# First scores by head halves: k on its own queue, all eight PSUM banks, and a new order for three batches

## The chip, the cores and the metric

The kernel runs on one core of a Trainium2 chip. The metric is device time in microseconds. A core has a matrix engine (TensorE, PE in the profile; its weight loads are PEld), a vector engine (VectorE, DVE), a scalar engine for functions of one argument (ScalarE, ACT), a general one (GpSimd, POOL) and one that only issues transfers (SyncE, SP). Each has its own queue of instructions and works through it in order. Semaphores make one wait for another. Matrix results go to PSUM, a memory of eight banks of 128 partitions x 512 FP32. Transfers from main memory are issued by GpSimd or by the sync queue and are carried out by 16 DMA engines.

## The reference

Causal attention with a window of 64 keys (batch 8, 8 heads, 576 positions, 64 columns a head), then a gated feed-forward layer (4608 tokens, 512 columns, 1536 hidden).

```python
scores = scale * np.matmul(q, k.transpose(0, 1, 3, 2))
rel = pos[:, None] - pos[None, :]
scores = np.where((rel >= 0) & (rel < 64), scores, -1e9)
scores = scores - np.max(scores, axis=-1, keepdims=True)
attn = np.exp(scores)
attn = attn / (np.sum(attn, axis=-1, keepdims=True) + 1e-09)
x = np.matmul(attn, v)              # heads side by side: [4608, 512]
out = (np.maximum(x @ w_gate, 0.0) * (x @ w_val)) @ w_out
```

## The kernel before

Attention is cut into 24 units of 192 query positions (three a batch), the feed-forward layer into 12 tiles of 384 tokens, two units each. A scheduler of its own fixes the order: `W.at(t, fn)` puts a piece of work on a heap, and while the feed-forward matmuls are emitted the clock `W.clock` moves and due pieces are emitted between them. The times `t` only order things; nothing waits for them on the chip.

Loads of q and k go over GpSimd's queue, which turns FP32 into FP16 on the way, one transfer for each half (`hh`) of the eight heads. VectorE transposes 32 x 32 blocks:

```python
def qk_load(b, name, hh):
    tile_ = nat[b, name, hh] = a_in.tile([128, S // 32 * D], FP16, name=f"{name}{hh}", bufs=2)
    src = (q if name == "q" else k)[b, G * hh:G * hh + G]
    nc.gpsimd.dma_start(tile_, src.rearrange("h (i j) d -> (h i) (j d)", i=32))

def qk_trans(b, name, hh):
    ...
    nc.vector.transpose(dst.rearrange("p (i j) -> p j i", i=32), src)
```

A unit: scores of four heads side by side on TensorE (`u_st`, the 64 columns of a head summed in two parts `dh`; both head halves in one bank), the exponential on ScalarE, the window mask as a product on VectorE (units 0 and 1 instead start from a large negative bias that TensorE adds, `u_bias`), P times V and the row sums on TensorE (`u_pv`), then the division:

```python
def u_st(u):
    ...
    for hh in range(2):
        for w in range(2):
            for dh in range(2):
                for g in range(G):
                    rows = slice(32 * g, 32 * g + 32)
                    nc.tensor.matmul(d["st"][g][:, (2 * hh + w) * 128:(2 * hh + w + 1) * 128],
                                     kT[rows, hh, ...], qT[rows, hh, ...], ...)

def u_exp(u, g):
    nc.scalar.activation(d["p"][g]..., d["st"][g], ACT.Exp, scale=scale)      # 512 columns

def u_copy(u, n):  nc.scalar.copy(d["xs"][:, c], d["pv"][c][:, 0])            # P times V, unnormalized
def u_sum(u, half): nc.vector.transpose(to[:, c], d["pv"][c][:, 1])           # row sums
def u_back(u):      # reciprocal, and transpose back
def u_norm(u):      nc.vector.tensor_tensor(xt[...], d["xs"], rs, MUL)
```

PSUM is held by two pools: `f_ps` with four tiles of one bank (tag "h") and `a_ps` with two tiles of two banks (tag "a"). Unit 0 scores into the four of `f_ps`, later units into `a_ps`. `heat(n)` issues n matmuls of zeros that keep TensorE active. The program:

```python
for name, hh in (("k", 0), ("k", 1), ("q", 0), ("q", 1)):
    qk_load(0, name, hh)
...
heat(12, units[1]["st"][0])
bands(); constants(); v_ones(1, nc.vector)     # masks on GpSimd, constants on VectorE
W.at(5.85, band_bias)
W.at(6.2, lambda: v_load(0)); W.at(6.3, lambda: v_load(1))
W.at(6.4, lambda: w_load(*G3[0], 15.0))        # then V3[0], G3[1], V3[1], G3[2], V3[2]
...
W.at(11.0, lambda: heat(8))
plan_unit(0, 10.2, ...); plan_unit(1, 10.8, ...); plan_unit(2, 24.0, *fast)
plan_unit(3, 45.3, *fast); plan_unit(4, 53.0); plan_unit(5, 60.5, *fast)
...
W.advance(15.7)
ready(1); hidden(0, 0, U, 0, 4, 4)             # projections of tile 0, tokens 0 to 191
ready(2); hidden(0, U, TT, 0, 4, 4)            # tokens 192 to 383
hidden(0, 0, TT, 4, NF, 4)
output_by_rows(0)
ready(3); hidden(1, 0, U); output(1, (0,))
ready(4); hidden(1, U, TT); output(1, (1, 2))
for t in range(2, NU // 2):
    ready(2 * t + 2); hidden(t, 0, TT)
    (output if t < NU // 2 - 1 else output_last)(t)
```

`hidden` makes the gate and value projections (512 columns of x against 128 of the weights, four matmuls a block), the relu on ScalarE and the product on VectorE; `output` the last projection.

Of the kernel before, what the change touches and what calls it, by code (L numbers as in the profile page):

```python
# [9 lines left out]
FP32 = mybir.dt.float32  # L10
FP16 = mybir.dt.float16
ACT = mybir.ActivationFunctionType
# [30 lines left out]
def kernel(  # L43
# [121 lines left out]
        src = (q if name == "q" else k)[b, G * hh:G * hh + G]  # L165
        nc.gpsimd.dma_start(tile_, src.rearrange("h (i j) d -> (h i) (j d)", i=32))

    def qk_trans(b, name, hh):

        src = nat.pop((b, name, hh)).bitcast(FP32).rearrange("p (j e) -> p j e", e=32)  # L170
        dst = qTs[b % 2][:, hh] if name == "q" else kTs[b % 2][:, hh, 64:64 + S]
        dst = dst.bitcast(FP32).rearrange("p c o -> p (c o)")
        nc.vector.transpose(dst.rearrange("p (i j) -> p j i", i=32), src)  # L173

    def v_load(u):
        b, uu = divmod(u, UB)
# [7 lines left out]

        nc.vector.tensor_copy(v16s[u % UB][0:64, 0, :, 0:64], v16s[u % UB - 1][64:128, 1, :, 0:64])

    def u_bias(u):

        d = units.setdefault(u, {})
        if "st" not in d:  # L190
            st_tiles(u)
        d["biased"] = True
        for g in range(G):
            nc.tensor.matmul(d["st"][g].rearrange("p (h c) -> p h c", h=2), ident,
                             bias.rearrange("p w c -> p (w c)")[:, None, :].to_broadcast([128, 2, 256]),
                             start=True, stop=False, skip_group_check=True)

    def heat(n, to=None):

        if to is None:  # L200
            to = f_ps.tile([128, 512], FP32, name="h0", tag="h")
        for _ in range(n):
            nc.tensor.matmul(to, zero[:, 0:128], zero, start=True, stop=True)  # L203

    def st_tiles(u):
        d = units.setdefault(u, {})
        if u == 0:
            d["st"] = [f_ps.tile([128, 512], FP32, name="st", tag="h") for _ in range(G)]
        else:
            halves = [a_ps.tile([128, 2, 512], FP32, name="st", tag="a") for _ in range(2)]  # L210
            d["st"] = [halves[g // 2][:, g % 2] for g in range(G)]

    def u_st(u):
        d = units.setdefault(u, {})
        kT, qT = kTs[(u // UB) % 2], qTs[(u // UB) % 2]
        biased = "biased" in d
        if not biased:
            st_tiles(u)
        ks = U * (u % UB)
        for hh in range(2):  # L220
            for w in range(2):
                for dh in range(2):
                    for g in range(G):
                        rows = slice(32 * g, 32 * g + 32)
                        nc.tensor.matmul(  # L225
                            d["st"][g][:, (2 * hh + w) * 128:(2 * hh + w + 1) * 128],
                            kT[rows, hh, ks + 128 * w:ks + 128 * w + 128, dh],
                            qT[rows, hh, ks + 64 * w:ks + 64 * w + 128, dh],
                            start=(dh == 0 and not biased), stop=(dh == 1),
                            skip_group_check=biased)  # L230
        d["p"] = [None] * G
        return 0.65

    def u_exp(u, g):
        d = units[u]
        d["p"][g] = a_p.tile([128, 2, 256], FP16, name="p")
        nc.scalar.activation(d["p"][g].rearrange("p h c -> p (h c)"), d["st"][g], ACT.Exp, scale=scale)  # L237

    def u_mask(u, g):
        p = units[u]["p"][g]  # L240
        nc.vector.tensor_tensor(  # L241
            p, p, mask.rearrange("p w c -> p (w c)")[:, None, :].to_broadcast([128, 2, 256]), MUL)

    def u_pv(u):
        if u > 1:
            return u_pv_wide(u)
        d = units[u]
        v16 = v16s[u % UB]
        if u == 0:
            d["pv"] = [f_ps.tile([128, 2, U], FP32, name="pv", tag="h") for c in range(NC)]  # L250
        else:
            halves = [a_ps.tile([128, 2, 512], FP32, name="pv", tag="a") for _ in range(2)]
            d["pv"] = [halves[c % 2][:, c // 2, 0:2 * U].rearrange("p (s c) -> p s c", s=2) for c in range(NC)]
        for c in (0, 2, 1, 3):
            for s in range(2):
                for w in range(2):
                    for e in range(2):
                        h = 2 * c + e
                        nc.tensor.matmul(
                            d["pv"][c][64 * e:64 * e + 64, s, 64 * w:64 * w + 128],  # L260
                            v16[:, w, h, 0:64] if s == 0
                            else (ones0 if u % UB == 0 and w == 0 else ones),
                            d["p"][h % G][:, h // G, 128 * w:128 * w + 128],
                            start=(s == 0 and w == 0), stop=(s == 1 and w == 1),
                            skip_group_check=True)
        return 1.2
# [18 lines left out]
    def u_copy(u, n):  # L285
        d = units[u]
        if "xs" not in d:
            d["xs"] = a_n.tile([128, NC, U], FP32, name="xv", bufs=2)
        if u < 2:
            c = (0, 2, 1, 3)[n]  # L290
            nc.scalar.copy(d["xs"][:, c], d["pv"][c][:, 0])
        else:
            for e in range(2):
                rows = slice(64 * e, 64 * e + 64)
                nc.scalar.copy(d["xs"][rows, n::2], d["pv"][n][rows, :, e, 0:U])  # L295

    def u_sum(u, half):
# [2 lines left out]
            d["sT"] = a_n.tile([128, NC, U // 32, 32], FP32, name="sT", bufs=1)  # L300
        to = d["sT"].rearrange("p g b c -> p g (b c)")
        if u < 2:
            for c in (half, half + 2):
                nc.vector.transpose(to[:, c], d["pv"][c][:, 1])
        else:
            for e in range(2):
                nc.vector.transpose(to[64 * e:64 * e + 64, half::2],  # L307
                                    d["pv"][half][64 - 64 * e:128 - 64 * e, :, e, 0:U])
# [138 lines left out]
                    out_evac(t, op, sub)  # L447

    with tc.manual_schedule():
        for name, hh in (("k", 0), ("k", 1), ("q", 0), ("q", 1)):  # L450
            qk_load(0, name, hh)
        warm = consts.tile([128, 2], FP32)
        nc.vector.memset(warm, 0.0)
        nc.scalar.activation(warm[:, 1:2], warm[:, 0:1], ACT.Exp)
        zero = consts.tile([128, 512], FP16)
        nc.vector.memset(zero, 0.0)
        st_tiles(1)
        heat(12, units[1]["st"][0])
        bands()
        constants()  # L460
        v_ones(1, nc.vector)
        W.at(5.85, band_bias)
        G3, V3, O3 = ([(wt, src, f0, f0 + 4) for f0 in (0, 4, 8)]
                      for wt, src in ((wg, moe_w_gate), (wv, moe_w_val), (wo, moe_w_out)))
        W.at(6.2, lambda: v_load(0))
        W.at(6.3, lambda: v_load(1))
        W.at(6.4, lambda: w_load(*G3[0], 15.0))
        W.at(6.5, lambda: w_load(*V3[0], 17.6))
        W.at(6.6, lambda: w_load(*G3[1], 20.2))
        W.at(9.9, lambda: w_load(*V3[1], 22.8))  # L470
        W.at(9.9, lambda: w_load(*G3[2], 25.4))
        W.at(9.9, lambda: w_load(*V3[2], 28.0))
        W.at(12.3, lambda: v_load(2))
        W.at(13.6, lambda: w_load(*O3[0], 32.5))
        W.at(13.7, lambda: w_load(*O3[1], 35.1))
        plan_batch(0, None, (4.5, 5.9, 7.3, 8.8))
        plan_batch(2, 37.6, (71.0, 72.4, 73.8, 75.2))
        plan_batch(1, None, (37.5, 39.0, 42.6, 44.0))
        W.at(13.8, lambda: qk_load(1, "k", 0))
        W.at(13.8, lambda: qk_load(1, "k", 1))  # L480
        W.at(13.9, lambda: w_load(*O3[2], 40.6))
        W.at(14.0, lambda: qk_load(1, "q", 0))
        W.at(14.0, lambda: qk_load(1, "q", 1))
        W.at(14.1, lambda: v_load(3))
        W.at(30.0, lambda: v_load(4))
        W.at(30.1, lambda: v_load(5))
        W.at(6.2, lambda: u_bias(0))
        W.at(6.3, lambda: u_bias(1))
        W.at(11.0, lambda: heat(8))
        W.at(13.5, lambda: v_before(1))  # L490
        W.at(21.0, lambda: v_ones(2, nc.vector))
        W.at(18.0, lambda: v_before(2))
        W.at(21.0, lambda: v_ones(0, nc.vector))
        W.at(22.0, k_zeros)
        fast = 0.8, 1.5, 3.9, (4.1, 5.3), (4.2, 5.4, 6.4, 7.5), 0.5
        plan_unit(0, 10.2, 0.7, None, 2.7, (4.4, 4.4, 4.4, 4.4), (3.4, 3.3, 4.2, 4.7), 0.5)
        plan_unit(1, 10.8, 2.1, None, 4.2, (5.2, 5.2, 5.3, 5.3), (4.7, 4.6, 5.0, 5.5), 0.5)
        plan_unit(2, 24.0, *fast)
        plan_unit(3, 45.3, *fast)
        plan_unit(4, 53.0)  # L500
        plan_unit(5, 60.5, *fast)
        T = 71.5
        early, late = (-7.4, -6.0, -4.6, -3.2), (-20.3, -18.9, -17.5, -16.1)
        for t in range(3, NU // 2):
            for u, at, tr in ((2 * t, T + 0.5, early), (2 * t + 1, T + 13.2, late)):
                if u % UB == 0 and u > 2 * UB:
                    plan_batch(u // UB, at + tr[0] - 10, [at + x for x in tr])
            plan_unit(2 * t, T + (6.5 if t == 3 else 0.5))
            plan_unit(2 * t + 1, T + (15.5 if t == 3 else 13.2), copy=(4.7, 5.8), norm=(4.8, 5.9, 6.9, 8.0))
            T += 26.525  # L510
        W.advance(15.7)
        ready(1)
        hidden(0, 0, U, 0, 4, 4)
        ready(2)
# [44 lines left out]
```

The softmax here doesn't subtract the row's maximum and nothing guards it: scores larger than these inputs give would overflow.

## Time and profile before

| what | value |
|---|---|
| median of three runs | 346.7 us (345.4 to 347.64) |
| span of the profiled execution | 346.2 us |
| TensorE busy | 331.1 us, 96% |
| VectorE busy | 250.7 us, 72% |
| ScalarE busy | 182.2 us, 53% |
| first projections of tile 0, tokens 0 to 191 | at 20.86 us |
| the same for tokens 192 to 383 | at 24.27 us |

In rows of the timeline the columns are start, length, engine, line, operation, what is written and read, the shape, and the count; in brackets the idle time ahead and what ended it. In the chain they are start, length, engine and work. Matmuls overlap each other, so that the length of a row exceeds what its instructions cost one after another; starts are safer to compare than busy times.

### The profile page before, as it was taken

What the parts mean: (1) busy time and instruction counts of PE and PEld (TensorE: products, weight loads), DVE (VectorE), ACT (ScalarE), POOL (GpSimd) and SP (SyncE); (2) the same over time, 40 slices, a digit from 0 to 9 for tenths busy, and PEclk for the clock granted to TensorE, in tenths of its full rate; (3) what the DMA queues carried; (4) which work ended last, traced back from release to release, by engine and by line L of the source; (5) the groups of instructions that cost most, each with busy time, mean ns of one, the idle gap of its engine ahead of it and who ended that gap; (6) DMA issues with size and microseconds to landing.
All of it is one profiled execution on the core that took longest, in us unless ns stands there. A gap on an engine that the chain in (4) does not pass through costs nothing.

```text
span 346.2 us, 7305 instructions
## 1 busy us (share of the span) xinstructions
PE 331.1 (96%) x2936; PEld 199.5 (58%) x2936; DVE 250.7 (72%) x450; ACT 182.2 (53%) x375; POOL 66.7 (19%) x101
## 2 busy tenths in 40 slices
PE   7669899999998999999999999999999999999996
PEld 2366467955654555655665655664664664664653
DVE  5397948897897883888879864878969964865430
ACT  1356346744755555565564565564664763763322
POOL 8822421420120410420120410420110200000000
PEclk9899999999999999999999999999999999999999
DMA  7999998790351951972333864665306501001002
GB/s 129 174 205 197 202 163 160 86 175 31 25 67 57 134 80 70 119 80 91 25 24 100 87 94 103 67 111 114 24 2 111 43 2 61 32 0 62 31 2 91
DMA packets 59666, 29.70 MB, mean 86 GB/s; under 512 B 46065, under 2 KB 51057, under 8 KB 59633
## 3 DMA queue, kind: packets, MB, share of 16 engines
q0 software_dynamic: 54160, 19.80, 52.5%
q1 hardware_dynamic: 5328, 9.37, 7.2%
q8 instruction: 23, 0.38, 0.5%
q14 instruction: 11, 0.08, 0.1%
q10 hardware_dynamic: 144, 0.07, 0.1%
HBM read 39.58 MB, written 9.44 MB: 142 GB/s over the span
## 4 chain that ended last, share of the span: by engine, by line
PE 81%; DVE 12%; DMA 2%; issue 2%; ACT 1%; POOL 1%; ACTq 0%; DVEq 0%; POOLq 0%
PE h L384 51%; PE op L398 20%; PE pv L277 5%; PE st L225 4%; DVE sT L307 2%; DMA q<-in_q_dram 2%; DVE qT L173 2%; DVE xt L322 2%; DVE kT L173 1%; DVE g_sb L372 1%; DVE rs L316 1%; PE h L203 1%; PE op L430 1%; DVE p L241 1%; ACT r_sb L369 1%
## 5 line engine op out<-in xcount | busy, mean ns | idle before, releaser
L384 PE MATMUL h<-xt,wg 128*128 128x384 f16 (+1 forms) x640 | 116.6, 310 | 3.9 <-DVE xt L322 3.9
L384 PE MATMUL h<-xt,wv 128*128 128x384 f16 (+1 forms) x640 | 116.6, 310 | 0.2 <-ACT r_sb L369 0.2
L372 DVE TENSOR_TENSOR g_sb<-r_sb,h 128x384 f16<-128x384 f32 x144 | 78.0, 548 | 36.5 <-PE h L384 30.6
L369 ACT ACTIVATE r_sb<-h 128x384 f32<-128x384 f32 x144 | 70.9, 496 | 56.2 <-PE h L384 48.8
L398 PE MATMUL op<-wo,g_sb 128*128 128x512 f16 x420 | 93.2, 379 | 1.3 <-DVE g_sb L372 0.8
L384 PEld LDWEIGHTS <-wg 128*128 128x128 f16 x640 | 59.4, 98 | 37.7 <-DVE xt L322 3.1
L384 PEld LDWEIGHTS <-wv 128*128 128x128 f16 x640 | 59.7, 98 | 32.2 <-issue 0.5
L181 POOL DMA_DIRECT2D v<-in_v_dram x48 | 40.4, 847 | 192.0 <-PE pv L277 185.0
L398 PEld LDWEIGHTS <-g_sb 128*128 128x128 f16 x420 | 40.9, 98 | 49.3 <-issue 1.7
L237 ACT ACTIVATE p<-st 128x512 f16<-128x512 f32 x96 | 52.1, 606 | 21.7 <-PE st L225 20.0
L307 DVE STREAM_TRANSPOSE sT<-pv 64x384 f32<-64x384 f32 x88 | 51.1, 580 | 11.5 <-PE pv L277 9.9
L405 ACT COPY o_sb<-op 128x512 f32<-128x512 f32 x35 | 20.5, 586 | 59.6 <-PE op L398 59.6
L241 DVE TENSOR_TENSOR p<-p,mask 128x512 f16<-128x512 f16 x88 | 34.0, 420 | 24.6 <-ACT p L237 24.6
L295 ACT COPY xv<-pv 64x384 f32<-64x384 f32 x88 | 41.6, 473 | 18.8 <-DVE sT L307 8.8
L316 DVE STREAM_TRANSPOSE rs<-rT 128x768 f32<-128x768 f32 x24 | 23.5, 978 | 0.8
L277 PE MATMUL pv<-p,v 128*128 128x128 f16 x352 | 23.7, 219 | 0.4 <-DVE p L241 0.3
L322 DVE TENSOR_TENSOR xt<-xv,rs 128x768 f16<-128x768 f32 x24 | 22.8, 948 | 1.3 <-DVE rs L316 0.5
L277 PEld LDWEIGHTS <-v 128*128 128x128 f16 x352 | 21.5, 98 | 3.3 <-DVE p L241 0.5
L173 DVE STREAM_TRANSPOSE kT<-k 128x576 f32<-128x576 f32 x16 | 19.6, 1244 | 2.0 <-DMA k<-in_k_dram 1.8
L173 DVE STREAM_TRANSPOSE qT<-q 128x576 f32<-128x576 f32 x16 | 19.1, 1241 | 2.2 <-DMA q<-in_q_dram 2.1
L225 PE MATMUL st<-qT,kT 32*128 32x128 f16 x768 | 16.2, 218 | 4.1 <-DVE qT L173 4.1
L225 PEld LDWEIGHTS <-kT 32*128 32x128 f16 x768 | 11.8, 94 | 11.7 <-issue 11.7
(45 smaller groups left out, 71.5 us busy)
## 6 DMA issues: line engine op xcount, KB each, us to landing
out_dram<-o_sb SPq DMA_DIRECT2D x35, 256.0 KB, 2.0
v<-in_v_dram POOLq DMA_DIRECT2D x38, 128.0 KB, 3.9
k<-in_k_dram POOLq DMA_DIRECT2D x16, 288.0 KB, 6.6
q<-in_q_dram POOLq DMA_DIRECT2D x16, 288.0 KB, 8.4
wg<-in_moe_w_gate_dram POOLq DMA_DIRECT2D x3, 512.0 KB, 10.9
wv<-in_moe_w_val_dram POOLq DMA_DIRECT2D x3, 512.0 KB, 12.7
wo<-in_moe_w_out_dram POOLq DMA_DIRECT2D x3, 512.0 KB, 17.1
v<-in_v_dram POOLq DMA_DIRECT2D x10, 64.0 KB, 3.3
```

The source lines that it names most:

```text
L173: nc.vector.transpose(dst.rearrange("p (i j) -> p j i", i=32), src)
L181: nc.gpsimd.dma_start(v16[p0:128, w, :, 0:64], v[b, :, k0 + p0:k0 + 128].rearrange("h p d -> p h d"))
L225: nc.tensor.matmul(d["st"][g][:, (2 * hh + w) * 128:(2 * hh + w + 1) * 128], kT[rows, hh, ks + 128 * w:ks + 128 * w + 128, dh], qT[rows, h ...
L237: nc.scalar.activation(d["p"][g].rearrange("p h c -> p (h c)"), d["st"][g], ACT.Exp, scale=scale)
L241: nc.vector.tensor_tensor(p, p, mask.rearrange("p w c -> p (w c)")[:, None, :].to_broadcast([128, 2, 256]), MUL)
L277: nc.tensor.matmul(d["pv"][c % 2][:, c // 2, e, 64 * w:64 * w + 128], v16[:, w, 128 * h - 64 * e:128 * h - 64 * e + 128], d["p"][h % G][:, ...
L295: nc.scalar.copy(d["xs"][rows, n::2], d["pv"][n][rows, :, e, 0:U])
L307: nc.vector.transpose(to[64 * e:64 * e + 64, half::2], d["pv"][half][64 - 64 * e:128 - 64 * e, :, e, 0:U])
L369: nc.scalar.activation(part(r_sb), part(h1), ACT.Relu)
L372: nc.vector.tensor_tensor(g_sb[:, f:f + w, c0:c1], part(r_sb), part(h2), MUL)
L384: nc.tensor.matmul(h[:, b * n:b * n + n], wt[:, c, (f + b) * 128:(f + b) * 128 + 128], xt[:, c, c0:c1], start=(c == 0), stop=(c == NC - 1))
L398: nc.tensor.matmul(op, g_sb[:, f, bass.ds(sub * 128, 128)], wo[:, f], start=(f == 0), stop=(f == NF - 1))
```

## The change

It is for the start of the kernel and for the first batches. Five parts:

- k of batch 0 comes as FP32 over the sync queue, beside q over GpSimd's. ScalarE rounds it to FP16 in two parts a head half, and VectorE transposes each part.
- Unit 0 is scored by head halves: half 0 into the four banks of `f_ps`, half 1 into the four of `a_ps`. Each half has exponentials of 256 columns. P times V of the first two column chunks needs only head half 0. Unit 1 takes two banks of each pool.
- Warming matmuls are 256 wide, accumulate zeros into the spare half of a bank, and lie between the bias and the scores of unit 0, no longer ahead of its P times V.
- The third piece of wo is loaded ahead of batch 1's k and q instead of between them.
- Later units are planned earlier, and transposes of batches 1 and 2 stand elsewhere: one k transpose of batch 2 now lies at 50.0, near unit 4.

The core of the diff:

```diff
+    def k_first(hh):
+        k32 = nat["k32", hh] = x_sb.tile([128, S // 32 * D], FP32, name="k32", bufs=2)
+        nc.sync.dma_start(k32, k[0, G * hh:G * hh + G].rearrange("h (i j) d -> (h i) (j d)", i=32))
+
+    def k_round(hh, part, parts):
+        n = S // 32 * D // parts
+        if part == 0:
+            nat[0, "k", hh] = a_in.tile([128, S // 32 * D], FP16, name=f"k{hh}", bufs=2)
+        nc.scalar.copy(nat[0, "k", hh][:, n * part:n * part + n], nat["k32", hh][:, n * part:n * part + n])
...
     def st_tiles(u):
...
         if u == 0:
-            d["st"] = [f_ps.tile([128, 512], FP32, name="st", tag="h") for _ in range(G)]
+            d["st"] = [[one("st") for _ in range(G)]]
+            halves = [two("st") for _ in range(2)]
+            d["st"].append([halves[g // 2][:, g % 2] for g in range(G)])
+        elif u == 1:
+            half = two("st")
+            d["st"] = [[half[:, 0], half[:, 1], one("st"), one("st")]] * 2
...
-        for name, hh in (("k", 0), ("k", 1), ("q", 0), ("q", 1)):
-            qk_load(0, name, hh)
+        for hh in range(2):
+            k_first(hh)
+        for hh in range(2):
+            qk_load(0, "q", hh)
...
+        for hh in range(2):
+            for part in range(2):
+                k_round(hh, part, 2)
+        W.at(5.0, lambda: qk_trans(0, "k", 0, 0, 9))
+        W.at(5.1, band_bias)
+        W.at(5.2, lambda: qk_trans(0, "k", 0, 9, 18))
+        W.at(7.0, lambda: qk_trans(0, "q", 0))
+        W.at(8.6, lambda: qk_trans(0, "k", 1, 0, 9))
+        W.at(8.7, lambda: qk_trans(0, "k", 1, 9, 18))
+        W.at(9.9, lambda: qk_trans(0, "q", 1))
...
-        W.at(13.7, lambda: w_load(*O3[1], 35.1))
-        plan_batch(0, None, (4.5, 5.9, 7.3, 8.8))
-        plan_batch(2, 37.6, (71.0, 72.4, 73.8, 75.2))
-        plan_batch(1, None, (37.5, 39.0, 42.6, 44.0))
-        W.at(13.8, lambda: qk_load(1, "k", 0))
-        W.at(13.8, lambda: qk_load(1, "k", 1))
-        W.at(13.9, lambda: w_load(*O3[2], 40.6))
-        W.at(14.0, lambda: qk_load(1, "q", 0))
+        W.at(12.7, lambda: w_load(*O3[1], 33.8))
+        W.at(12.8, lambda: w_load(*O3[2], 36.4))
+        plan_batch(1, None, (37.5, 39.0, 40.4, 41.8))
+        W.at(13.0, lambda: qk_load(1, "k", 0))
...
-        W.at(11.0, lambda: heat(8))
+        W.at(5.3, lambda: u_bias(0))
+        W.at(5.4, lambda: heat(10, units[0]["spare"], False))
+        W.at(8.7, lambda: u_st(0, (0,)))
+        W.at(9.5, lambda: heat(8, units[0]["spare"], False))
+        W.at(11.0, lambda: u_st(0, (1,)))
+        for g in range(G):
+            W.at(9.6 + 0.05 * g, lambda g=g: u_exp(0, g, 0))
+            W.at(11.1 + 0.05 * g, lambda g=g: u_exp(0, g, 1))
+            W.at(12.0 + 0.05 * g, lambda g=g: u_copy(0, g))
+            W.at(12.3 + 0.05 * g, lambda g=g: u_exp(1, g))
+        W.at(11.4, lambda: u_pv(0, (0, 1)))
+        W.at(11.45, lambda: u_bias(1, (2, 3)))
+        W.at(11.5, lambda: u_pv(0, (2, 3)))
+        W.at(11.6, lambda: u_bias(1, (0, 1)))
+        W.at(11.7, lambda: u_st(1))
+        W.at(11.9, lambda: u_sum(0, 0))
...
-        plan_unit(3, 45.3, *fast)
-        plan_unit(4, 53.0)
-        plan_unit(5, 60.5, *fast)
-        T = 71.5
+        plan_unit(3, 42.5, *fast)
+        plan_unit(4, 50.0)
+        plan_unit(5, 58.0, *fast)
+        T = 68.4
...
-                if u % UB == 0 and u > 2 * UB:
+                if u == 2 * UB:
+                    plan_batch(2, 36.9, (50.0, T + 0.3, T + 1.7, T + 3.1))
+                elif u % UB == 0:
                     plan_batch(u // UB, at + tr[0] - 10, [at + x for x in tr])
-            plan_unit(2 * t, T + (6.5 if t == 3 else 0.5))
-            plan_unit(2 * t + 1, T + (15.5 if t == 3 else 13.2), copy=(4.7, 5.8), norm=(4.8, 5.9, 6.9, 8.0))
+            plan_unit(2 * t, T + (5.0 if t == 3 else 0.5))
+            plan_unit(2 * t + 1, T + 13.2, copy=(4.7, 5.8), norm=(4.8, 5.9, 6.9, 8.0))
...
-        W.advance(15.7)
+        W.advance(13.7)
```

## The prediction

> **What bounds the kernel now.** I began with the chain that ended last, by share of the span, because it says at once which engine sets the time.
>
> ```profile
> PE 81%; DVE 12%; DMA 2%; issue 2%; ACT 1%; POOL 1%; ACTq 0%; DVEq 0%; POOLq 0%
> ```
>
> Four fifths are TensorE. That part is a steady stream of projections and can't be shortened by a reordering, so what the change can win lies in the other fifth. The chain in order of time, from 0 to 41 us, shows where the biggest piece of it is (start, length, what):
>
> ```profile
> 3.04 8.03 DMA q<-in_q_dram
> 11.10 1.27 DVE qT L173
> 12.41 1.23 PE st L225 x48
> 13.64 3.09 PE h L203 x8
> 16.73 0.36 PE pv L259 x8
> 17.12 1.19 DVE sT L304 x4
> 18.33 0.32 DVE rT L314
> 18.67 0.99 DVE rs L316
> ...
> 19.76 0.96 DVE xt L322
> ```
>
> The second q half lands at 11.07; then follow its transpose, the scores, eight warming matmuls, P times V, and VectorE's normalization. The third view, the timeline, tells when projections start, for tokens 0 to 191 and then for 192 to 383:
>
> ```profile
> 20.86 1.48 PE L384 MATMUL h<-xt,wg 128*128 128x192 f16 x16 [1.69 <-DVE xt L322]
> ...
> 24.27 1.49 PE L384 MATMUL h<-xt,wg 128*128 128x192 f16 x16 [0.61 <-DVE xt L322]
> ```
>
> So 24.27 us pass before TensorE has all of tile 0 to work on, with only 192 tokens of the first four column blocks done by then. The fourth view, TensorE's own timeline after that, shows what else it loses:
>
> ```profile
> 40.26 7.93 PE L398 MATMUL op<-wo,g_sb 128*128 128x512 f16 x36 [0.82 <-DVE g_sb L372]
> ...
> 58.19 0.59 PE L398 MATMUL op<-wo,g_sb 128*128 128x512 f16 x2 [0.52 <-ACT r_sb L369]
> ...
> 71.14 0.82 PE L277 MATMUL pv<-p,v 128*128 128x128 f16 x8 [0.31 <-DVE p L241]
> ...
> 106.31 0.82 PE L384 MATMUL h<-xt,wg 128*128 128x384 f16 x4 [1.57 <-DVE xt L322]
> ```
>
> I compared starts with the sum of the instructions ahead of them (a 384-column matmul each 0.163 us, a score tile 0.57, a P-times-V group 0.90). Between 24.27 and 106.31 TensorE loses 1.3 us by 40.26, 0.7 by 58.7, 0.8 by 72.8 and 1.5 at 106.31: 4.3 us. After 106.31 I find nearly nothing.
>
> **What the Trainium skill says.** "DMA: Bandwidth & Descriptors", section "SWDGE vs HWDGE vs iDMA": a transfer that changes the type must be issued by GpSimd. So k on the sync queue arrives as FP32, and an engine has to round it. The same page, "Issuing engines are not separate DMA queues": all issuers share the 16 DMA engines. The trace agrees that these are busy: share 1.06 over the first 11 us. A second queue therefore shortens GpSimd's issuing and starts data earlier, but makes no bandwidth. "ScalarE: Activation LUTs", section "What ACT_TABLE_LOAD costs": 186 ns + 0.833 ns a column, about 93 ns overlapped between neighbours. For 512 columns that gives 613 and 520 ns; the trace has 600 ns for one and 3.05 us for six, 508 each. It agrees, so I use it for 256 columns: 306 ns each in a row, an estimate. "TensorE: Matmul & The Clock Gate", section "What's actually happening": the clock halves after an idle window of some 3.4 us and returns after a busy one. Here eight warming matmuls took 3.15 us, 0.39 each, and the granted clock was 0.50 from 13 to 16 us, after TensorE had been almost idle from 8.3 to 12.4. It agrees.
>
> **Part 1, loads.** GpSimd issues q at 1.31 instead of at 2.52; k goes beside it. Its mask work moves up by the two issues removed (2 x 0.62 = 1.2 us), and so do the v and weight issues. Bytes read up to the second q stay the same: four of 590 KB, which at twice the 195 GB/s that the windows show (they count the FP16 written) take 1.5 us each. Before, the first k landed at 5.05, the first q at 8.55, the second at 11.07. If the two queues share and the sync queue starts 0.5 us sooner, I put k half 0 at 4.9, q half 0 at 6.5 to 7, k half 1 at 7.8, q half 1 at 9.5 to 10 (it was the last of four before too, and v's small packets delayed it). ScalarE's rounding is four copies of 576 columns, by the same formula 0.57 us each, and VectorE transposes in halves of 0.63; both are done by about 10. What ends last remains q half 1: at 9.9, 1.2 us earlier.
>
> **Part 2, unit 0.** From q half 1 the new path is: transpose 1.27 (row above) and 0.05 of waiting; 16 score matmuls 0.4; four exponentials of 256 columns 1.3, against four of 512 at 2.05 before; so all weights of unit 0 exist 3.1 us after landing, at 13.0. Head half 0 has been scored and exponentiated in the wait, and the first two P-times-V chunks run beside the second half's exponentials. The eight 512-column warming matmuls are gone from this place. Before, the exponentials of unit 0 ended near 14.9 (12.84 + 2.05), yet P times V began at 16.66: the warming cost 1.8 us. The new 256-column ones lie in the wait for q.
>
> After 13.0: the ScalarE queue does copies of the first chunks, then VectorE's last two row sums, about 1.45 us; reciprocal 0.33, back transpose 1.0, xt 1.0: xt(0) at 16.8. On TensorE, scores of unit 1 are issued behind the P times V of unit 0; its exponentials follow the four copies, about 14.75, and last 2.05; its P times V comes ahead of the projections in the queue and ends at 17.6. So projections start at 17.6, not 20.86: 3.3 us. Unit 1's row sums (1.2), reciprocal, back transpose and xt end at 20.6, and the first two projection groups (2.8 us) fill nearly all of that time. Tile 0 is complete at 20.65 against 24.27: **3.6 us**. The weights: the first gate and value pieces were in by 16.7 and 19.5 (GpSimd's waits); 1.2 us earlier they are just in time.
>
> **Part 3, batch 1 and after.** The last wo piece ahead of batch 1 changes nothing in the total to land: wo was needed 5.2 us after 40.26, and q of batch 1 landed near 45, over 4 us before unit 3's scores at 50.43. The order after keeps some 2 us of that. What matters is VectorE, in the order in which the built kernel issues its instructions. Unit 7 moves up, its P times V now precedes the 36 output matmuls (7.8 us), and two rather than three transposes lie ahead of its xt. Row sums 2.4, two transposes 2.5, one product 0.55, normalization 2.3: 7.75 us in 8.4. The 1.5 us at 106.31 should go. But one batch-2 k transpose, 1.25 us, now lies ahead of unit 4's four mask products. In the trace those end 8.3 us after unit 3's P times V starts; with the transpose some 9.2, where TensorE comes after 7.4 to 8.1. I put the stalls there at 1.35, instead of 0.7, and at unit 5 at 1.0, instead of 0.8. At the first output group I leave 1.4: the gate products still queue on VectorE behind row sums and xt. Sum 3.8 against 4.3: **0.4 us** won.
>
> Sum: 3.6 + 0.4 = 4.0, less 0.1 for issue costs not seen: 346.7 - 3.9 = **342.8 us**.
>
> **Rivals.** (a) Weights become the bound. The DMA engines work without pause from 3 to 50 us, and the value piece for the first group lands at 18.2 by my estimate where 19.0 is needed. If the loads win only 0.3 us, TensorE waits 0.5 there: about 343.5. Speaking for it: share over 1 in every window; against: later pieces lead their use by 5 us before and by over 2 after. (b) Two queues interleave, q half 1 lands at 11 as before: then only the structure counts, 2.4 + 0.4: 343.9. (c) TensorE is cold when projections start, since it idles from about 14.5 to 16.9: half speed for up to 3 us, 1.5 us lost, about 344.3. Against: an idle 1.7 us ahead of 20.86 left the clock at 1.00. (d) Unit 4's masks cost nothing, because VectorE idles before them more than I count, and all later stalls go: 341. (e) VectorE's blocked queue spreads the stall to units 5 and 6: 345.
>
> **Range and chances.** The prologue is worth 2.4 to 4.3 by (a) to (c), the middle -1.2 to 2 by (d) and (e). Together 340.5 to 345.5. Faster by over 2% needs 6.9 us: 0.06. Slower by over 2% needs a new wait of 11 us that I see nowhere: 0.01.
>
> **What would show it.** Right: projections start at 17 to 18, tile 0's second half at 20 to 21.3, no idle above 0.3 us ahead of tile 4's first projections, P times V of unit 4 waiting on the mask product by up to 1 us, and the work from there as long as before, 239.9 us. Wrong: q landing after 10.5; a wait on a wv load; clock below 0.9 after 17 us; an op wait of over 2 us near 37; exponentials of 256 columns above 0.35 us apart.

## The result and the profile after

The changed kernel takes 342.81 us (median of four runs, 342.74 to 344.84), the kernel before in the same comparison 347.1 (345.4 to 347.64). The ratio is 0.9896, with an interval of 0.9852 to 0.994: faster by 1.0%. The prediction said 342.8, so the sum was right. The terms were not all right, and the profile shows it at once. Its span is 343.1 us, against 346.2 before.

On the page of the changed kernel, the chain that ended last by engine is still four fifths TensorE (80%, before 81%), and VectorE has a point less (11%, before 12%).

```profile
PE 80%; DVE 11%; issue 4%; DMA 2%; POOL 1%; ACT 1%; ACTq 0%; DVEq 0%; POOLq 0%
```

The timeline of the changed kernel, start of the program:

```profile
7.21 1.26 DVE L184 STREAM_TRANSPOSE qT<-q 128x576 f32<-128x576 f32 x1 [0.80 <-DMA q<-in_q_dram]
...
9.66 1.26 DVE L184 STREAM_TRANSPOSE qT<-q 128x576 f32<-128x576 f32 x1
...
10.97 0.41 PE L246 MATMUL st<-qT,kT 32*128 32x128 f16 x16 [1.06 <-DVE qT L184]
...
11.41 1.21 ACT L262 ACTIVATE p<-st 128x256 f16<-128x256 f32 x4 [1.26 <-PE st L246]
...
12.08 0.29 PE L287 MATMUL pv<-p,v 128*64 128x128 f16 x2 [0.52 <-DMA v<-in_v_dram]
...
13.91 0.42 PE L287 MATMUL pv<-p,v 128*64 128x128 f16 x4
...
19.08 1.50 PE L412 MATMUL h<-xt,wg 128*128 128x192 f16 x16
...
22.31 1.49 PE L412 MATMUL h<-xt,wg 128*128 128x192 f16 x16 [0.41 <-DVE xt L350]
```

q half 1 is transposed at 9.66 instead of 11.10, and the four exponentials end at 12.62. So far the prediction holds (9.9 and 13.0). Then the chain loses time: P times V waits for v until 12.08, and four of its matmuls take 0.42 us from 13.91 on. In the kernel before four took less:

```profile
16.91 0.28 PE L259 MATMUL pv<-p,v 128*64 128x128 f16 x4
```

Projections start at 19.08 and 22.31, where 17.6 and 20.65 were predicted. The stages of the two kernels, by busy time of each engine and the granted TensorE clock (PEclk), tell why. The kernel before:

```profile
8.00:12.00 4.00, 0.73 (x18) 0.36 (x17) 2.16 (x2) 0.00 (x0) 4.00 (x6) 1.00 2.43 144
12.00:16.00 4.00, 3.59 (x54) 1.83 (x54) 0.65 (x2) 3.05 (x6) 3.17 (x5) 0.59 1.39 188
```

The changed kernel:

```profile
8.00:12.00 4.00, 2.09 (x44) 1.45 (x42) 2.80 (x4) 1.80 (x7) 3.80 (x6) 1.00 2.65 136
12.00:16.00 4.00, 3.92 (x52) 2.03 (x54) 1.80 (x5) 1.58 (x6) 2.49 (x4) 0.57 1.25 206
```

The first busy column is TensorE; PEclk is the third number from the right. In both kernels the clock falls to about 0.58 from 12 to 16 us, after a stretch in which TensorE waited for q. This execution of the changed kernel did not escape it. Most others did: the runs list the mean granted clock, and the four at 0.998 to 1.000 have spans of 341.0 to 341.1; only the profiled one has 0.995 and 343.1.

After the start, the lines of TensorE's timeline that answer to those of the kernel before:

```profile
38.57 1.02 PE L426 MATMUL op<-wo,g_sb 128*128 128x512 f16 x4 [0.22 <-DVE g_sb L400]
39.90 6.20 PE L426 MATMUL op<-wo,g_sb 128*128 128x512 f16 x28 [0.31 <-DVE g_sb L400]
...
49.46 0.42 PE L246 MATMUL st<-qT,kT 32*128 32x128 f16 x16 [0.37 <-DVE qT L184]
...
61.28 1.39 PE L305 MATMUL pv<-p,v 128*128 128x128 f16 x16
...
70.53 0.49 PE L305 MATMUL pv<-p,v 128*128 128x128 f16 x6 [0.35 <-DVE p L266]
...
103.41 0.81 PE L412 MATMUL h<-xt,wg 128*128 128x384 f16 x4
```

The idle 1.57 us ahead of tile 4's first projections is gone. From 22.31 to 103.41 it takes 81.10 us, before (24.27 to 106.31) 82.04. From there to the end it takes 239.7, before 239.9: little happened there.

### The profile page after: what moved, and what is told of

It reads as the page before. It is cut to its first block, busy times and chain, and to the rows that moved or that the text cites. A ratio compares the mean times of both kernels' runs of the same rounds, so it can differ in the third digit from the quotient of the medians.

```text
span 343.1 us, 7364 instructions
## 1 busy us (share of the span) xinstructions
PE 332.7 (97%) x2950; PEld 201.2 (59%) x2950; DVE 251.5 (73%) x452; ACT 186.7 (54%) x383; POOL 65.7 (19%) x99
## 4 chain that ended last, share of the span: by engine, by line
PE 80%; DVE 11%; issue 4%; DMA 2%; POOL 1%; ACT 1%; ACTq 0%; DVEq 0%; POOLq 0%
PE h L412 48%; PE op L426 21%; PE pv L305 6%; DVE sT L335 3%; PE st L246 3%; DVE g_sb L400 2%; DMA v<-in_v_dram 2%; DVE qT L184 2%; DVE xt L350 1%; DVE rs L344 1%; DVE p L266 1%; DVE kT L184 1%; PE op L458 1%; PE pv L287 1%; PE st L206 1%
## 5 line engine op out<-in xcount | busy, mean ns | idle before, releaser
L260 ACT ACTIVATE p<-st 128x512 f16<-128x512 f32 x92 | 49.9, 604 | 11.6 <-PE st L246 11.4
L184 DVE STREAM_TRANSPOSE kT<-k 128x576 f32<-128x576 f32 (+1 forms) x18 | 19.8, 1119 | 1.9 <-ACT k L177 1.8
```

The source lines that it names most:

```text
L184: nc.vector.transpose(dst.rearrange("p (i j) -> p j i", i=32)[:, j0:j1], src[:, j0:j1])
```

## The experiments

Two theories that the profile leaves open. A, mine: the earlier q and the scoring by head halves shorten the start, and unit 7's place the middle. D: much of the gain is that TensorE's clock is halved less often during the wait for q. Then the kernels must be compared at the same clock. In the text below "full clock" means runs with a mean granted clock above 0.996, "halved" those with 0.995 or less; nearly all of the difference lies in the first 24 us. The kernel before, in 68 runs that accompany the experiments, was halved in 45, with a median span of 345.4, and at full clock in 23, with 343.6 (one more run, slow at 348.8, is left out). The changed kernel: 341.1 at full clock (four), 343.1 halved (one). Spans at full clock of one kernel spread by up to 1.1 us.

**start_only.** The changed start, and the order of the kernel before from the first projections of tokens 192 to 383:

```diff
-        plan_unit(3, 42.5, *fast)
-        plan_unit(4, 50.0)
-        plan_unit(5, 58.0, *fast)
-        T = 68.4
+        plan_unit(3, 43.3, *fast)
+        plan_unit(4, 51.0)
+        plan_unit(5, 58.5, *fast)
+        T = 69.5
```

(and unit 2, units 6 and 7, the transposes and the weights' planned times likewise, each 2.0 below the kernel before, so that TensorE's order is that of the kernel before).

> The changed kernel's start (k on the sync queue, unit 0 by head halves, warming matmuls moved), but from the first projection of the second token half on TensorE's order is that of the kernel before. Theory A (the start carries the gain, the middle under 1 us): about 343.7, 3.0 to 3.6 us below the kernel before, with a stall of some 1.5 us ahead of tile 4's first projections back. Rival B (the start gives back its gain to a cold TensorE and to the wait for v; the middle carries it): 345.5 or more.

343.92 us, ratio 0.9927 (0.9902 to 0.9951). Full clock 342.0 (five), 1.6 us below the kernel before; halved 343.5 (one). In its profile, whose clock was 1.00, projections of the second half start at 20.26, and the stall is back, on TensorE's timeline:

```profile
20.26 1.50 PE L412 MATMUL h<-xt,wg 128*128 128x192 f16 x16 [0.41 <-DVE xt L350]
...
102.27 0.82 PE L412 MATMUL h<-xt,wg 128*128 128x384 f16 x4 [1.57 <-DVE xt L350]
```

Theory A's number. The start does carry most of it, but at equal clock less than the 3.0 to 3.6 that A gave it.

**middle_only.** The start before, the order after, and wo ahead of batch 1:

```diff
-        T = 71.5
+        T = 70.4
...
-                if u % UB == 0 and u > 2 * UB:
+                if u == 2 * UB:
+                    plan_batch(2, 38.9, (52.0, T + 0.3, T + 1.7, T + 3.1))
+                elif u % UB == 0:
...
-            plan_unit(2 * t, T + (6.5 if t == 3 else 0.5))
+            plan_unit(2 * t, T + (5.0 if t == 3 else 0.5))
```

(units 2 to 5 and 7 likewise.)

> The kernel before's start, and the changed kernel's order on TensorE from there on, with wo ahead of batch 1. Theory A: 0.4 to 0.9 us below the kernel before, so about 346.3. Rival B: 2 us or more below.

345.85 us, ratio 0.9972 (0.9956 to 0.9988). Full clock 342.9 (seven), 0.7 below; halved 344.4 (15), 1.0 below. So 15 of 22 were halved, as often as in the kernel before: the share goes with the start. The two parts nearly add at full clock: 1.6 + 0.7 = 2.3, against 2.5 together. Against the nine full-clock runs of the same comparison alone (343.9) they are 1.9 and 1.0, so such differences are good to some 0.3 us.

**warm.** More work for TensorE in its waits:

```diff
-        W.at(9.5, lambda: heat(8, units[0]["spare"], False))
+        W.at(9.5, lambda: heat(18, units[0]["spare"], False))
...
-        W.at(11.45, lambda: u_bias(1, (2, 3)))
+        for _ in range(2):
+            W.at(11.3, lambda: u_bias(1, (2, 3)))
```

> The changed kernel with 18 instead of 8 warming matmuls in the wait for the second q half, and with the bias of unit 1's last two banks issued twice and ahead of unit 0's first P times V, where TensorE waits for v. Theory A: the granted clock stays at 1.00 from 12 to 16 us (0.50 to 0.61 in the profile of the changed kernel), P times V of unit 0 and the scores of unit 1 run at full speed, the second token half starts at 20.3 to 20.8 instead of 22.31, and the profiled span is 341.0, 2 us below that of the changed kernel's profile; the median, about 342.8, hardly moves, because its other runs were warm already. Rival: the clock makes no difference because v and ScalarE set the time; then the second half starts at 22 again.

343.45 us, ratio 0.9907 (0.9884 to 0.993). Clock 1.00 from 12 to 16 us and the second half at 20.90, 1.41 earlier than the halved profile of the changed kernel; the rival's 22 is out. But the full-clock span is 341.6, 0.5 above the changed kernel's. The doubled bias ended at 12.3 and P times V came behind it, 1.31 us after half 1's scores began (11.01 to 12.32); in start_only it came 0.35 after them.

**k_gpsimd.** k of batch 0 as before:

```diff
-        for hh in range(2):
-            k_first(hh)
-        for hh in range(2):
-            qk_load(0, "q", hh)
+        for name, hh in (("k", 0), ("k", 1), ("q", 0), ("q", 1)):
+            qk_load(0, name, hh)
...
-        for hh in range(2):
-            for part in range(2):
-                k_round(hh, part, 2)
```

> The changed kernel, but k of batch 0 again over GpSimd's queue, in FP16, with no rounding on ScalarE; the rest as changed. Theory A (the sync queue is worth the 1.4 us that q lands earlier): q half 1 lands at 11 and the time is 1.0 to 1.6 us above the changed kernel, 344.0. Rival C (the 16 DMA engines are the bound, so v of unit 0 lands when it landed and the wait for it takes the place of the wait for q): under 0.5 us above, 343.2.

343.79 us, ratio 0.992 (0.9891 to 0.9948). Full clock 342.0 (five): 0.9 above the changed kernel. q half 1 is transposed at 10.95 here and at 9.66 in the changed kernel's profile, but single executions differ by as much: wo_back, with the changed kernel's loads, has it at 10.67. So the runs decide, and the rival's 0.5 is too small. The sync queue is worth about 0.9 us.

**before_warm.** The kernel before, kept busy in its wait (the first part lies in `u_st`):

```diff
         for hh in range(2):
+            if u == 0 and hh == 1:
+                u_bias(1)
+                u_bias(1)
...
-        W.at(6.3, lambda: u_bias(1))
+        for _ in range(3):
+            W.at(6.3, lambda: u_bias(1))
```

> The kernel before, with TensorE kept busy while it waits for q: the bias of unit 1 is issued five times instead of once (two extra ahead of unit 0's scores, two between its head halves), into the same banks, so that nothing else changes. Theory D (in the kernel before the clock is halved from 12.8 to 16.8 us in most executions, the eight warming matmuls then take 3.15 us instead of 1.7 and delay P times V, and 1.5 to 2 us of the change's gain are just that it is halved less often): granted clock 1.00 in the profile, second token half at 22.3 to 22.8 instead of 24.27, span 343.6 to 344.2, median 345.4. Rival A (the exponentials and the order set the start): second half at 23.7 or later, median 346.5 or more.

346.71 us, ratio 1.0018 (1.0006 to 1.0029). A miss for D's number, and instructive. Its warming matmuls and first P times V on TensorE's timeline:

```profile
13.56 1.89 PE L203 MATMUL h<-zero 128*128 128x512 f16 x8 [0.22 <-ACT p L240]
15.37 0.30 PE L262 MATMUL pv<-p,v 128*64 128x128 f16 x4
```

Its stages:

```profile
12.00:14.00 2.00, 1.78 (x54) 1.03 (x53) 0.26 (x1) 1.09 (x3) 2.00 (x4) 1.00 1.29 178
14.00:16.00 2.00, 2.00 (x29) 1.10 (x29) 0.17 (x1) 1.95 (x4) 1.56 (x3) 1.00 1.24 206
16.00:18.00 2.00, 1.54 (x50) 1.26 (x44) 1.93 (x6) 1.89 (x6) 0.38 (x1) 1.00 1.24 206
18.00:20.00 2.00, 0.43 (x5) 0.44 (x6) 1.89 (x5) 0.08 (x1) 0.74 (x1) 0.96 1.24 206
20.00:22.00 2.00, 2.00 (x14) 1.84 (x13) 1.83 (x5) 1.46 (x5) 0.17 (x1) 0.50 1.24 207
```

The clock is full where it was halved before, and P times V starts at 15.37 instead of 16.66: by the starts, the eight warming matmuls take 1.8 us instead of 3.1. Then the wait for xt leaves TensorE at 0.43 of 2 us, and the clock is halved from 20 us on, under the projections. Nine of 22 runs were halved (345.7). At full clock (13) it takes 344.8, 1.2 above the kernel before. The added bias is in the way: in its profile q half 1 is transposed from 9.92 to 11.18, but half 1's scores, behind the bias in TensorE's order, start at 12.47. So this run shows what the clock does to the warming matmuls; it does not show what the clock alone costs the kernel before.

**late_half0** and **late_half0b.** Head half 0 not scored ahead, and its exponentials later too. The first edit:

```diff
-        W.at(8.7, lambda: u_st(0, (0,)))
+        W.at(10.95, lambda: u_st(0, (0,)))
...
-            W.at(9.6 + 0.05 * g, lambda g=g: u_exp(0, g, 0))
+            W.at(11.02 + 0.01 * g, lambda g=g: u_exp(0, g, 0))
```

> The changed kernel, but head half 0 of unit 0 is scored only when q half 1 has landed, ahead of half 1, and its exponentials with it. Theory A (scoring by halves takes four exponentials, 1.2 us, off the path from q): 1.0 to 1.3 us above the changed kernel, 343.9. Rival (P times V waits for v until 11.6 to 12 anyway, which hides most of them): under 0.6 above.

343.66 us, ratio 0.9922 (0.9893 to 0.995). The edit did not do what it was for: half 0's scores stood behind the first warming matmuls only and still ran at 8.91. Its full-clock span is 341.1 (three), that of the changed kernel, and three of six were halved. The second edit puts half 1's scores first in the order:

```diff
-        W.at(8.7, lambda: u_st(0, (0,)))
+        W.at(11.005, lambda: u_st(0, (0,)))
...
-            W.at(9.6 + 0.05 * g, lambda g=g: u_exp(0, g, 0))
+            W.at(11.02 + 0.01 * g, lambda g=g: u_exp(0, g, 0))
```

> The changed kernel, with both head halves of unit 0 scored only when q half 1 has landed: half 1's scores first in TensorE's order, so that half 0 can't go ahead. All eight exponentials of 256 columns then follow in a row. Theory A (scoring by halves takes four exponentials, 1.2 us, off the path from q): 1.0 to 1.4 us above the changed kernel where the clock is the same, span 342.0 to 342.5 at full clock. Rival (P times V waits for v anyway, which hides most of them): under 0.6 above, below 341.7.

345.05 us, ratio 0.9924 (0.9896 to 0.9952; the kernel before took 347.06 there). Full clock 342.1 (three): 1.0 above the changed kernel. Four of seven were halved, at 343.5. So half of the work ahead of q half 1 saves 1.0 us, and fills TensorE's wait too.

**no_heat8.** The eight warming matmuls between the score halves left out:

```diff
-        W.at(9.5, lambda: heat(8, units[0]["spare"], False))
```

> The changed kernel without the eight warming matmuls between the two score halves of unit 0; nothing waits for them, so they cost no time of their own. Theory D (a wait of TensorE that lasts long enough decides whether the clock is halved, and the change wins by making it rarer): TensorE is idle from about 8.9 to 11 us, the clock is halved in most runs (mean granted clock 0.995 or less), the spans lie near 343.1 in most, near 341.0 in the others, median 344.5 or more. Rival (the warming there makes no difference): most spans at 341.0, as in the changed kernel.

343.91 us, ratio 0.9912 (0.988 to 0.9944). Seven of eight runs were halved (median span 342.3), one was not (340.6). With the start unchanged otherwise, 6 of 36 runs were halved (the changed kernel, start_only, k2_back, u7_late, wo_back and better). This settles the main point of D: 1 us of matmuls on zeros, for which nothing waits, decides how often the clock falls. D's median of 344.5 or more was too high: at either clock this kernel is not above the changed one, so what the matmuls buy is only the share.

**k2_back.** The first k transpose of batch 2 after unit 5 again, and unit 6 later:

```diff
-                    plan_batch(2, 36.9, (50.0, T + 0.3, T + 1.7, T + 3.1))
+                    plan_batch(2, 36.9, (T - 1.1, T + 0.3, T + 1.7, T + 3.1))
...
-            plan_unit(2 * t, T + (5.0 if t == 3 else 0.5))
+            plan_unit(2 * t, T + (6.5 if t == 3 else 0.5))
```

> The changed kernel, but the first k transpose of batch 2 stands again with the three others after unit 5, and unit 6 comes 1.5 us later in the order, as in the kernel before. Theory A (that transpose ahead of unit 4's masks costs 0.6 to 0.8 us on TensorE, and unit 7's new place alone removes the stall at tile 4): 0.4 to 0.7 us below the changed kernel, 342.2. Rival E (VectorE has no other room: with four transposes after unit 5 the stall comes back at unit 6 or 7): same or above, 342.8 to 344.

343.51 us, ratio 0.9924 (0.9901 to 0.9947). All six at full clock, 341.8: 0.7 above. Unit 4's P times V starts 1.33 us after the projections ahead of it instead of 1.51 and takes 1.06 instead of 1.39, so 0.5 us is won there. From 80 us on TensorE waits for:

```profile
PE st L246 <- DVE sT L335: 0.5, 1, 0.5
PE st L246 <- ACT xv L323: 0.4, 1, 0.4
PE pv L305 <- DVE p L266: 0.2, 1, 0.2
```

The changed kernel has none of these three waits from 75 us on. That is rival E: the work has to stand somewhere. The 1.1 us of waits belong to both parts of this edit, the transpose after unit 5 and the later unit 6; they were not tried apart.

**u7_late.** Unit 7 alone at its old place:

```diff
-            plan_unit(2 * t + 1, T + 13.2, copy=(4.7, 5.8), norm=(4.8, 5.9, 6.9, 8.0))
+            plan_unit(2 * t + 1, T + (15.5 if t == 3 else 13.2), copy=(4.7, 5.8), norm=(4.8, 5.9, 6.9, 8.0))
```

> The changed kernel with unit 7 alone at its old place, 2.3 us later in the order: its P times V lies behind eight output matmuls, and three transposes ahead of its xt. Theory A: 1.2 to 1.6 us above the changed kernel, 344.2, all of it in one idle time ahead of tile 4's first projections. Rival: under 0.5, because with one k transpose of batch 2 gone VectorE is no longer late.

343.76 us, ratio 0.9937 (0.9914 to 0.996). Full clock 342.05 (six): 0.95 above, and one new idle time:

```profile
103.02 0.82 PE L412 MATMUL h<-xt,wg 128*128 128x384 f16 x4 [1.25 <-DVE xt L350]
```

**wo_back.** The third wo piece between k and q of batch 1 again:

```diff
-        W.at(12.8, lambda: w_load(*O3[2], 36.4))
...
         W.at(13.0, lambda: qk_load(1, "k", 1))
+        W.at(13.0, lambda: w_load(*O3[2], 36.4))
         W.at(13.0, lambda: qk_load(1, "q", 0))
```

> The changed kernel with the third piece of wo loaded between k and q of batch 1 again, TensorE's order the same. Theory A (both are there long before they are needed): the same as the changed kernel within 0.3 us, 341.0 at full clock, 342.8. Rival: q or wo comes late, over 0.5 us above or below.

343.04 us, ratio 0.9892 (0.9848 to 0.9936); full clock 341.1 (five). That part of the change does nothing. Its start is the changed one, and its profile was taken at full clock, with the second half at 21.22.

**better.** Two transposes moved:

```diff
-        plan_batch(1, None, (37.5, 39.0, 40.4, 41.8))
+        plan_batch(1, None, (37.5, 39.0, 40.4, 40.45))
...
-                    plan_batch(2, 36.9, (50.0, T + 0.3, T + 1.7, T + 3.1))
+                    plan_batch(2, 36.9, (46.0, T + 0.3, T + 1.7, T + 3.1))
```

> The changed kernel with two transposes moved and TensorE's order the same: the last q transpose of batch 1 ahead of a gate product that waits for ScalarE (it held up unit 3's scores by 0.37 us), and the first k transpose of batch 2 into VectorE's idle time of 0.9 us ahead of unit 3's row sums, not ahead of unit 4's masks. Theory A: 0.37 us, and some 0.3 to 0.6 us at unit 4 and unit 5, are won: 0.5 to 0.9 below the changed kernel, span 340.2 to 340.6 at full clock, median 342.1. Rival E (VectorE's work between units 3 and 5 is the bound, wherever the transpose stands): 0.2 to 0.4 below at most.

343.1 us, ratio 0.9889 (0.9856 to 0.9923); full clock 341.3 (four): nothing won. The first move works: unit 3's scores no longer wait. The second falls on a transfer, on VectorE's timeline:

```profile
51.70 1.26 DVE L184 STREAM_TRANSPOSE kT<-k 128x576 f32<-128x576 f32 x1 [1.32 <-DMA k<-in_k_dram]
```

k of batch 2 had not landed. VectorE waited 1.32 us in order, its row sums came late, and unit 4's scores waited for the P times V buffer of unit 3, which ScalarE and VectorE had still to read:

```profile
55.27 0.79 PE L246 MATMUL st<-qT,kT 32*128 32x128 f16 x32 [1.40 <-ACT xv L323]
```

The idle time of 0.9 us was no room, because its data had not landed yet.

## Why the prediction was right, and where it wasn't

The landing of q differs between executions, and spans carry that with them. Two distances in the traces do not: from half 1's scores of unit 0 to the projections of the second token half, and from there to the end of the span (us).

| profile | clock, 12 to 16 us | scores to second half | second half to end |
|---|---|---|---|
| before | halved | 11.86 | 321.9 |
| changed | halved | 11.34 | 320.8 |
| start_only | full | 9.54 | 321.7 |
| wo_back | full | 9.27 | 320.8 |
| k_gpsimd | full | 9.33 | 320.7 |
| warm | full | 9.89 | 320.7 |
| late_half0b | full | 10.60 | 320.8 |
| u7_late | full | 9.26 | 321.8 |
| k2_back | full | 9.40 | 321.4 |
| better | full | 9.26 | 321.4 |

- **Loads.** The transpose of q half 1 was put 1.2 us earlier and came 1.4 earlier in the two profiles. But its start varies: 9.19 to 10.67 in the ten profiles with the new loads, 9.92 to 11.65 in the four with k over GpSimd; by the runs the gain is about 0.9. k half 1 was put at 7.8 and was there by 5.8 (7.0 in wo_back): the sync queue's two k halves came ahead of q, they did not share evenly with it. The rounding, put at 0.57 a part, took 0.63 and lay off the path. "What ends last remains q half 1" was wrong in most executions: in eight of the ten, VectorE starts q half 1 only 2.18 or 2.19 us after q half 0, behind the two transposes of k half 1. In wo_back:

```profile
8.49 1.26 DVE L184 STREAM_TRANSPOSE qT<-q 128x576 f32<-128x576 f32 x1 [2.23 <-DMA q<-in_q_dram]
9.59 1.24 DVE L184 STREAM_TRANSPOSE kT<-k 128x288 f32<-128x288 f32 x2
10.67 1.24 DVE L184 STREAM_TRANSPOSE qT<-q 128x576 f32<-128x576 f32 x1
```

There q half 1 had landed by about 9.9 (an estimate: issued at 2.0, 7.9 us to landing), 0.8 us before its transpose. Transposes of k half 1 ahead of q half 0 were not tried.
- **Scoring by halves.** Four exponentials were put at 1.3 us and took 1.21. The halves are worth 1.0 us at full clock by the spans, 1.3 by the table (late_half0b against wo_back).
- **Warming.** This term failed: "the warming cost 1.8 us". It was read off a profile of the kernel before in which the clock was halved; the same eight take 1.8 us instead of 3.1 when it isn't. So the start's 3.6 us compared a halved run of before with a full-clock run of after. Between the two halved profiles it is 2.0 (24.27 to 22.31), between full-clock spans 1.6. The path after the change was worked out well: 341.1 less 320.8 puts the second half at 20.3 in a typical full-clock run (an estimate), where 20.65 was predicted.
- **The clock, rival (c).** I placed it at the projections, at up to 1.5 us, and argued it away. It sits at 12 to 16 us, where the changed kernel waits for q and v. It costs 2.0 us by spans (343.1 against 341.1) and by the table (11.34 against 9.3), with the wait for v in it, though not in most runs.
- **v.** P times V of unit 0 waited a further 0.52 us for v in the changed kernel's profile and 0.21 in late_half0's, the two halved profiles with this start; no full-clock profile lists this wait. It was in none of the rivals.
- **The middle.** 0.4 us predicted, 0.94 between the profiles up to tile 4's first projections and 1.1 up to the end, which middle_only's profile has in full (320.8). Unit 7's stall, put at 1.5, was 1.3 by the profiles (72.79 to 106.31 before, 71.19 to 103.41 after, for the same work) and 0.95 by u7_late. The moved k transpose costs some 0.5 at unit 4, where 0.65 was put; unit 5's wait is 0.35 us, before 0.31, not 0.2 more. Unit 3's scores wait 0.37 for a transpose that stands behind a gate product: missed. better, which mended that, loses 0.6 after the start by the table, so its 341.3 owes something to an early q.
- **wo.** Nothing, as predicted.

The sum then has three parts: 2.5 us at equal full clock (343.6 to 341.1), of which 1.1 come from the middle and so about 1.4 from the start, and up to 1.8 us because the median run of the kernel before was halved (345.4 against 343.6) and the median run after is not. That is 4.3, by the medians of spans as by the run times. An estimate for the last part from the kernel before's own trace: the warming matmuls 1.3 longer than at full clock, the 48 score matmuls some 0.3 longer (1.17 by the starts, against 0.87 in before_warm), so 1.6. Parts removed one at a time (0.9 for the sync queue, 1.0 for the halves, 0.95 for unit 7) need not add up to the whole. The prediction's 3.9 came from a term that stood for the halving without naming it: that the number was right is in part luck.

Open: why a given run is halved. The share fell from 45 of 68 to 6 of 36 with the changed start; no_heat8 and late_half0b raise it to 7 of 8 and 4 of 7. That ties it to what TensorE does in the wait for q. What limit applies, the runs don't show. The idle window that the prediction names does not describe it: in the changed kernel's profile TensorE was busy 2.09 us of the 4 before the clock fell, and its longest idle time there was 1.06. Profiles with about as little, or less, stayed at full clock (no_heat8 2.26, wo_back 2.00, late_half0b 1.60).

## What to carry to other kernels

Before a term is read off one profile, look at the granted clock of that stage and at the runs' mean clocks: work that takes 3.1 us at half clock can be 1.8 us at full clock, and a change can win by making the halving rarer. Splitting the work that waits for the last transfer, so that half of it runs ahead, took 1.0 us off the path here. Before a transfer is called last, look at what stands ahead of its consumer in the queue. And an idle stretch of an engine is no room for a piece whose data land later; look up the landing first.

## What was not expected of the hardware

One microsecond of matmuls on zeros moved the share of half-clock runs from 6 of 36 to 7 of 8. Filling one wait moved the halving to the next one: the clock of before_warm was 1.00 from 12 to 16 us and 0.50 from 20 to 22. The landing of q half 0 differs between executions of the same start: its transpose began at 7.21 us in the changed kernel and at 8.49 in wo_back, and the scores of half 1 at 10.97 and 11.95.
